# A recurrent attention and four-expert layer on one core: the second chunk's first half goes to seven block products

## The chip, the cores and the metric

The kernel runs on one core of a Trainium2 chip. A core has five engines that each work through their own list of instructions in order: TensorE (PE in the profile; its weight loads stand apart as PEld), VectorE (DVE), ScalarE (ACT), GpSimd (POOL) and SyncE (SP), which here only issues transfers. Transfers (DMAs) run on 16 DMA engines; SP and POOL each feed a queue of them. On-chip memory is SBUF; TensorE writes its results to eight banks of PSUM, and the other engines read them from there. The metric is device time in microseconds (us) of the whole program, the median of several runs.

## The reference, cut to what matters

First a recurrence over the sequence, per batch and head, with gates between 0 and 1; then four experts, weighted by normalised probabilities. All of x is the output of the recurrence, with the heads laid side by side.

```python
f = 1.0 / (1.0 + np.exp(-f_logit))            # B=4, H=8, S=768, D=48
for t in range(S):
    state = f[:, :, t, :, None] * state + np.einsum('bhd,bhe->bhde', k[:, :, t], v[:, :, t])
    y[:, :, t] = np.einsum('bhd,bhde->bhe', q[:, :, t], state)
x = y.transpose(0, 2, 1, 3).reshape(B * S, H * D)        # 3072 x 384
p = domain_probs / (domain_probs.sum(-1, keepdims=True) + 1e-09)
for e in range(4):                                       # w1: 384 x 1024, w2: 1024 x 384
    out += p[:, e:e + 1] * (np.maximum(x @ w1[e], 0.0) @ w2[e])
```

## The kernel before

**Tiles and stages.** The sequence is cut into six chunks of 128 steps (`C = 6`, numbered 0 to 5). A chunk of all four batches gives 512 tokens (`NT`), 128 of each batch. For each chunk the kernel runs an attention part, which gives y of 128 tokens by 384 for each batch, and then the experts on those 512 tokens. Attention of chunk c+1 is woven into the experts of chunk c.

**Attention** (function `attention`) has, per chunk c and batch b, these steps, whose names are used below: `gate1`, `gate2` (ACT), `cs c.b` (running sums of the log gates, PE line L319), `exps` (ACT, L339), `q` and `k` (products with the exponentials, on DVE in the first six batches, else on POOL, L347), `tp` (their transposes: on PE with a copy out of PSUM, L356, or by a transposing DMA, L360), `at` (scores, PE, L383), `ev_at0`, `ev_at1` (masking, DVE, L387), `y` (PE, L394 and L398), `kv` and `ev_kv` (the state, PE L404 and DVE L411) and `sf` (the state's decay, POOL, L416 and L419).

**From y to the experts there are two ways.** In the plain way (chunk 0, and batches 0 and 1 of chunk 1) y is cast to bf16 (`ev_y`), transposed on PE (`xt`, L423), copied out of PSUM to the tile `x` (`ev_xt`), and goes through `h` (first layer, PE L432; relu L441 or L443) and `o` (second layer, PE L447, 8 matmuls of 384 columns for 128 tokens and one expert; `ev_o`, L454, scales by the probability and adds). In the other way (everything from batch 2 of chunk 1 on) the probability is put on y first: since it isn't negative, it passes through the relu. `ev_ys` (ACT L370 or DVE L372) writes y times the probability of one expert; `xs c.b.p` (SP, L375) transposes the two scaled copies of expert pair p by DMA. The first layer is `hs` (PE L464, six matmuls of 256 columns a step, 16 steps for a half chunk and both pairs), its relu `relu_s` (L470, L472). The second layer of two experts is then one product of a 2x2 block matrix (two batches by two experts) with another, and it is done with seven block products instead of eight: `p c.hf.p.m` (PE L501, m = 1 to 7, 8 matmuls of 192 columns each), from sums of hidden blocks `s1` to `s4` (DVE, L482) and sums of weight blocks `t p.1` to `t p.4` (DVE, L491; `t p.3` overwrites a part of the second layer's weights of expert 2p, so all `o` steps of that expert must be done before). `ev_p` (ACT L272 or DVE L509) adds the results up. `store` (SP, L513) writes 128 tokens out. The constant `FAST` (line 166) holds the first chunk and half that go this second way.

**What sets the order.** The program isn't written in its final order. Each step is entered with a cost, a priority and what it depends on; `Plan.run` (line 92) then walks through a model of the engines and fixes, once, in which order each engine gets its instructions and on which of two engines a step runs. Priorities come from the place in the loops and from the long string `MOVES` at the top, which shifts single steps (`name=shift`) or pins their engine (`@DVE`). On the chip every engine takes its instructions strictly in that order. Up to the first `h` the empty time of PE is filled with dummy matmuls (L873).

**The start.** SP loads f, k, q of chunk 0; POOL issues its v (L278) and the weights (L291) in eleven pieces: piece 0 and 1 are the two halves of expert 0's first layer, 2 and 3 those of expert 1, 4 and 5 the second layer of expert 0, and so on. The first expert's first layer in chunk 0 runs in eight units of 12 matmuls with 128 columns, one batch at a time. The weave of chunk 1's attention begins at priority `u0 + 12`.

Of the kernel before, what the change touches and what calls it, by code (L numbers as in the profile page):

```python
# [15 lines left out]
    "k 0.2=46.8@DVE;at 0.1=35.2;ev_xt 0.0=109.8@DVE;ev_at1 0.1=70.1;ev_y 0.3=27.8@ACT;cs 1.0=11.6;at 1.1=19.4;ev_xt 1.0=-4.1@DVE;"  # L16
    "y 1.1=-37.1;ev_ys 1.2.1.1=-9.1;ev_kv 1.3=70.1;ld q2.0=-1.5;ld k2.2=0.2;ld v2.2=15.3;relu 0.0.0.0=-7.7@DVE;h 0.0.0.256=-53.5;"
    "h 0.0.4.256=16.5;o 0.0.0.1=5.7;h 0.1.3.0=25.3;o 0.0.1.1=45.6;o 0.0.3.0=67.2;o 0.1.3.1=6.9;relu 0.3.2.0=15.9@DVE;h 0.3.3.0=-4.2;"
    "h 0.3.6.0=-15.8;o 0.2.3.0=-0.7;h 0.3.7.0=377.1;o 0.2.3.1=-2.5;tp 2.3=-3.5;at 2.1=1.3;ev_ys 2.0.0.0=-60.4@ACT;xs 2.0.1=-2.5;"
    "ev_at0 2.1=-36;ev_at0 2.2=23.5;xs 2.3.0=11.1;kv 2.0=-27.5;sf 2.0.1=-9.9;sf 2.0.3=-58.7;ld f3.0=3.2;o 0.3.1.1=10.5;o 0.3.3.0=-6.7;"  # L20
    "o 0.3.3.1=-22.1;store 0.3.0=20.5;h 1.1.3.0=2.6;o 1.0.1.1=-1;h 1.2.4.0=8.1;h 1.2.5.0=43.5;h 1.3.0.0=-9.1;o 1.2.0.0=19.1;"
    "relu 1.3.1.0=-6.8@ACT;o 1.2.1.0=1.8;h 1.3.3.0=10.5;relu 1.3.7.0=7@DVE;hs 1.1.1.0.0=-39.6;hs 1.1.1.0.4=-28.6;egs 3.1=26.2;"
    "tp 3.1=-56.1;q 3.2=2.6;ev_at0 3.1=7.2;ev_ys 3.1.0.1=20.9;ev_kv 3.0=13.3;kv 3.2=18.7;kv 3.3=10.8;ld q4.0=-7;ld k4.2=14.4;"
    "p 1.1.1.5=-1.3;ev_p 1.1.1.5=-31.6;store 1.2.0=32.2;p 1.1.1.4=5.8;s1 2.0.0=-10.2;hs 2.0.1.0.0=7;relu_s 2.0.1.0.4=1.8@ACT;"
    "p 2.0.0.4=-14.9;s1 2.0.1=2.2;hs 2.1.0.0.0=-31.7;ev_p 2.0.1.1=-60.4;ev_p 2.0.1.2=4.7;hs 2.1.0.0.2=-47.5;relu_s 2.1.0.1.2=2.4@ACT;"
    "hs 2.1.0.0.4=0.4;p 2.0.1.7=10.9;ev_p 2.0.1.3=-15.8;hs 2.1.0.1.6=-2.8;s1 2.1.0=-39.4;s2 2.1.0=2.3;p 2.1.0.1=1.8;p 2.1.0.2=56.5;"
    "ev_p 2.1.0.6=-15.4@DVE;p 2.1.0.5=-1.9;hs 2.1.1.1.6=-3;relu_s 2.1.1.1.6=9.4@DVE;s3 2.1.1=-18;cs 4.0=-6.9;egs 4.0=1.1;q 4.0=0.6;"
    "v 4.1=-4.6;tp 4.1=-14.2;cs 4.2=-65.6;cs 4.3=-4.7;ev_ys 4.0.0.1=-2.9@DVE;ev_ys 4.1.1.0=-89;ev_ys 4.2.1.1=0@ACT;ev_at0 4.3=55.1;"
    "ev_kv 4.1=52.4;kv 4.2=12.3;ld k5.0=7.4;ld f5.2=7.3;ld k5.2=-22.8;hs 3.0.0.0.2=1.4;relu_s 3.0.0.0.2=0@ACT;p 2.1.1.6=17.2;"
    "p 2.1.1.4=17.3;s4 3.0.0=8.2;relu_s 3.0.1.1.0=31.3@DVE;ev_p 3.0.0.2=-39.3;relu_s 3.0.1.0.2=36.2@DVE;p 3.0.0.5=2.3;hs 3.0.1.0.4=2.5;"  # L30
    "relu_s 3.0.1.1.4=8.8@ACT;p 3.0.0.4=3.4;hs 3.0.1.1.6=-5.6;relu_s 3.0.1.1.6=-12.6@DVE;p 3.0.1.1=7.7;hs 3.1.0.1.0=4.3;p 3.0.1.2=0.6;"
    "hs 3.1.0.0.4=-3.5;hs 3.1.0.1.6=2.1;s1 3.1.0=-4.1;s2 3.1.0=-28.8;s3 3.1.0=13.5;hs 3.1.1.0.0=0.4;relu_s 3.1.1.0.0=0@DVE;"
    "hs 3.1.1.1.0=-32.5;hs 3.1.1.1.2=5.9;relu_s 3.1.1.0.4=6.7@DVE;s1 3.1.1=10.8;s2 3.1.1=-19.8;gate1 5.2=-24.6;cs 5.2=-43.5;cs 5.3=10.3;"
    "ev_at0 5.0=-17.9;ev_at1 5.0=-18.3;ev_ys 5.0.0.0=0.1@DVE;ev_ys 5.0.0.1=18.3@DVE;ev_ys 5.1.0.0=-2.7@DVE;ev_ys 5.1.1.0=31.5@DVE;"
# [19 lines left out]
class Plan:  # L54
# [37 lines left out]
    def run(self):  # L92
# [3 lines left out]
        for o in self.ops:  # L96
            if o.name.split(" ")[-1].startswith("0.") and set(o.costs) & {"ACT", "DVE"}:
                o.lag += 0.1
# [41 lines left out]
def kernel(  # L140
# [12 lines left out]
    B, H, S, D = q.shape  # L153
    assert (B, H, S, D) == (4, 8, 768, 48)
    T = 128
# [5 lines left out]
    E, Din, F = moe_w1.shape  # L161
# [383 lines left out]
    for i, (e, which, ks, cols) in enumerate(pieces):  # L545
# [10 lines left out]
        if i == 0:  # L556
            add_v(B - 2, -459.6)
            add_v(B - 1, -459.5)
# [354 lines left out]
```

## Time and profile before

| what | us |
|---|---|
| median of 3 runs (288.75 to 288.84) | 288.76 |
| the profiled execution | 288.44 |
| its span, first to last instruction | 286.7 |
| PE busy, in the span | 280.0 |
| DVE / ACT / POOL busy | 195.5 / 180.7 / 112.0 |
| granted TensorE clock, mean | 1.000 |

The page of a profile gives busy times of each engine, the span cut into 40 slices, the chain of work that ended last (followed back from the last instruction, at each step to what released it), and groups of equal instructions with count, total and mean. A timeline lists instructions in order of time: start, duration, engine, line, operation, output and inputs, shape, and in brackets the idle time before with what ended it. Durations of matmuls there contain the pipeline; from start to start they are shorter, so costs of PE work are taken from the chain, where n matmuls in a row stand with the time that they held the chain.

### The profile page before, as it was taken

What the parts mean: (1) busy time and instruction counts of PE and PEld (TensorE: products, weight loads), DVE (VectorE), ACT (ScalarE), POOL (GpSimd) and SP (SyncE); (2) the same over time, 40 slices, a digit from 0 to 9 for tenths busy, and PEclk for the clock granted to TensorE, in tenths of its full rate; (3) what the DMA queues carried; (4) which work ended last, traced back from release to release, by engine and by line L of the source; (5) the groups of instructions that cost most, each with busy time, mean ns of one, the idle gap of its engine ahead of it and who ended that gap; (6) DMA issues with size and microseconds to landing.
All of it is one profiled execution on the core that took longest, in us unless ns stands there. A gap on an engine that the chain in (4) does not pass through costs nothing.

```text
span 286.7 us, 7475 instructions
## 1 busy us (share of the span) xinstructions
PE 280.0 (98%) x3010; PEld 235.7 (82%) x3016; DVE 195.5 (68%) x385; ACT 180.7 (63%) x343; POOL 112.0 (39%) x181
## 2 busy tenths in 40 slices
PE   7999999999999999999999999999999999999994
PEld 2567555567786999998999999999999999998994
DVE  4595122778698868846889876888885787630683
ACT  5847683758776846867695657375865544659500
POOL 5796500218763762478157258134373000000000
PEclk9999999999999999999999999999999999999999
DMA  7999999997998989999889999995254143420011
GB/s 154 206 173 206 207 195 201 181 198 167 176 184 161 213 154 211 128 222 195 177 182 171 126 219 179 222 184 112 58 132 90 28 84 83 88 56 2 2 55 55
DMA packets 157782, 41.85 MB, mean 146 GB/s; under 512 B 148124, under 2 KB 156956, under 8 KB 157748
## 3 DMA queue, kind: packets, MB, share of 16 engines
q1 hardware_dynamic: 146500, 34.66, 63.7%
q0 software_dynamic: 11248, 6.72, 16.5%
q8 instruction: 23, 0.38, 0.6%
q14 instruction: 11, 0.09, 0.1%
HBM read 31.51 MB, written 4.72 MB: 126 GB/s over the span
## 4 chain that ended last, share of the span: by engine, by line
PE 93%; SPq 2%; DMA 2%; DVE 1%; issue 0%; ACT 0%; DVEq 0%
PE ps_m L464 33%; PE ps_m L501 29%; PE ps_m L447 11%; PE ps_m L432 11%; SPq L282 2%; PE ps_m L383 2%; PE ps_m L398 2%; DMA q<-in_q_dram 2%; PE ps_m L394 1%; PE ps_m L404 1%; PE ps_m L319 1%; PE ps_m L356 1%; DVE AT L387 0%; ACT QK L272 0%; PE ps_m L423 0%
## 5 line engine op out<-in xcount | busy, mean ns | idle before, releaser
L464 PE MATMUL ps_m<-x,w_sb 128*128 128x256 bf16 x864 | 105.6, 273 | 0.0
L472 ACT ACTIVATE h<-ps_m 128x512 bf16<-128x512 f32 x113 | 67.2, 598 | 45.3 <-PE ps_m L464 35.9
L464 PEld LDWEIGHTS <-w_sb 128*128 128x128 bf16 x864 | 82.9, 98 | 9.1
L501 PEld LDWEIGHTS <-S 128*128 128x128 bf16 x576 | 48.6, 98 | 1.1
L509 DVE TENSOR_TENSOR o<-ps_m,o 128x192 f32<-128x192 f32 x91 | 31.2, 354 | 20.0 <-PE ps_m L501 17.7
L482 DVE TENSOR_TENSOR S<-h 128x1024 bf16<-128x1024 bf16 x36 | 28.2, 800 | 13.0 <-ACT h L472 12.9
L501 PEld LDWEIGHTS <-h 128*128 128x128 bf16 x432 | 36.3, 98 | 0.9
L447 PE MATMUL ps_m<-w_sb,h 128*128 128x384 bf16 x192 | 36.1, 326 | 0.0
L432 PE MATMUL ps_m<-x,w_sb 128*128 128x128 bf16 (+2 forms) x260 | 35.6, 281 | 0.2
L443 ACT ACTIVATE h<-ps_m 128x512 bf16<-128x512 f32 (+1 forms) x49 | 24.6, 512 | 14.0 <-PE ps_m L432 12.9
L387 DVE TENSOR_TENSOR AT<-ps_m,mask 128x512 bf16<-128x512 f32 x48 | 30.5, 683 | 4.1 <-PE ps_m L383 3.8
L419 POOL TENSOR_TENSOR Sf<-Sf,egs 48x192 f32<-48x192 f32 x40 | 20.7, 521 | 28.4 <-DVE Sf L411 23.9
L339 ACT ACTIVATE e<-ps_m 128x384 f32<-128x384 f32 x48 | 26.9, 671 | 6.3 <-PE ps_m L319 2.9
L470 DVE TENSOR_SCALAR h<-ps_m 128x512 bf16<-128x512 f32 x31 | 21.0, 691 | 12.9 <-PE ps_m L464 10.3
L432 PEld LDWEIGHTS <-w_sb 128*128 128x128 bf16 x264 | 21.8, 98 | 9.4
L347 POOL TENSOR_TENSOR qk<-q,e 128x384 bf16<-128x384 f32 x19 | 24.1, 1271 | 13.7 <-ACT e L339 6.3
L501 PE MATMUL ps_m<-ts_sb,S 128*128 128x192 bf16 x288 | 28.7, 246 | 0.0
L501 PE MATMUL ps_m<-w_sb,S 128*128 128x192 bf16 x288 | 28.5, 246 | 0.0
L501 PE MATMUL ps_m<-w_sb,h 128*128 128x192 bf16 x288 | 28.4, 246 | 0.0
L447 PEld LDWEIGHTS <-h 128*128 128x128 bf16 x192 | 18.3, 98 | 11.9 <-issue 0.4
L370 ACT ACTIVATE yb<-ps_m,pn 128x384 bf16<-128x384 f32 x49 | 26.1, 584 | 2.8 <-PE ps_m L398 2.7
L347 POOL TENSOR_TENSOR qk<-k,e 128x384 bf16<-128x384 f32 x19 | 19.4, 1023 | 14.7 <-DVE Sf L411 4.0
(74 smaller groups left out, 308.7 us busy)
## 6 DMA issues: line engine op xcount, KB each, us to landing
out_dram<-o SPq DMA_DIRECT2D x23, 192.0 KB, 2.2
w_sb<-in_moe_w_dram POOLq DMA_DIRECT2D x5, 768.0 KB, 17.3
k<-in_k_dram SPq DMA_DIRECT2D x10, 384.0 KB, 5.5
q<-in_q_dram SPq DMA_DIRECT2D x10, 384.0 KB, 5.6
v<-in_v_dram SPq DMA_DIRECT2D x10, 384.0 KB, 5.6
f<-in_f_logit_dram SPq DMA_DIRECT2D x9, 384.0 KB, 4.9
w_sb<-in_moe_w_dram POOLq DMA_DIRECT2D x6, 384.0 KB, 8.7
f<-in_f_logit_dram SPq DMA_DIRECT2D x6, 192.0 KB, 3.8
```

The source lines that it names most:

```text
L339: nc.scalar.activation(out=o, in_=i, func=AF.Exp, scale=1.0 if j else -1.0)
L347: return engines[eng].tensor_tensor(out=tl("qk", c, b)[:, j, :, 0:D].rearrange("t (i r) d -> t i r d", r=2), in0=tl("qk"[j], c, b // 2)[:, ...
L370: nc.scalar.activation(out=ys, in_=y, func=AF.Copy, scale=pe)
L387: nc.vector.tensor_tensor(out=tl("AT", c, b)[:, r].rearrange("s i t -> s (i t)"), in0=tl("A", c, b, r).rearrange("s i t -> s (i t)"), in1= ...
L432: nc.tensor.matmul(out=hp(c, e, fc, n0, n1, nf)[:, f], lhsT=w1_sb[:, e, kk, (fc + f) * 128:(fc + f + 1) * 128], rhs=tl("xT", c)[:, kk, n0: ...
L443: nc.scalar.activation(out=dst, in_=src, func=AF.Relu)
L447: nc.tensor.matmul(out=tl("op", c, e, nt, part)[:, cols], lhsT=tl("h", c, e, half_of(c, nt * T))[:, fc, nt * T:(nt + 1) * T], rhs=w2_sb[:, ...
L464: nc.tensor.matmul(out=out_[:, f], lhsT=w1_sb[:, e, kk, (fc + f) * 128:(fc + f + 1) * 128], rhs=tl("xs", c, hf, p)[:, el, kk, :], start=(k ...
L472: nc.scalar.activation(out=dst, in_=tl("hp", c, hf, p, el, fc), func=AF.Relu)
L482: return nc.vector.tensor_tensor(out=s(j), in0=in0, in1=in1, op=op)
L501: nc.tensor.matmul(out=out_, lhsT=lhs[:, fc, :], rhs=rhs[:, fc, :], start=(first and fc == 0), stop=(fc == KF - 1), skip_group_check=True)
L509: nc.vector.tensor_tensor(out=o, in0=src, in1=o, op=ALU.add)
```

## The change

Four things change besides the priorities.

1. `FAST` becomes `(1, 0)`: batches 0 and 1 of chunk 1 also take the second way. Their `ev_y`, `xt` and `ev_xt` go, eight `ev_ys` and four `xs` come. The loop for chunk 1 issues two more groups of 16 `hs` steps in place of 32 `h` units of 256 columns, 14 block products in place of the 16 `o` steps of two halves each, and `t_sums()` before them all.
2. The first expert's first layer in chunk 0 runs in batches of two, one and one: hidden blocks 0 to 3 for batches 0 and 1 together (256 columns), then for batch 2, blocks 4 to 7 for batches 0 to 2 together (384 columns), then all for batch 3.
3. v of batch 2 is issued before the first weight piece instead of after it; the weave of chunk 1's attention starts at `u0 + 6`; a delay of 0.1 that the model put on ACT's and DVE's steps of chunk 0 is gone.
4. `MOVES` is another string from beginning to end (it is left out here but for a line), so the order differs on every engine in every chunk. Among others the loads of chunk 1's second half come as f, q, v, k instead of f, k, q, v; `k 0.0` and `q 0.1` move from POOL to DVE; and the last two block products and stores at the end change places.

```diff
 MOVES = (
-    "k 0.2=46.8@DVE;at 0.1=35.2;ev_xt 0.0=109.8@DVE;ev_at1 0.1=70.1;ev_y 0.3=27.8@ACT;cs 1.0=11.6;at 1.1=19.4;ev_xt 1.0=-4.1@DVE;"
+    "ld q1.2=-2.1;ld v1.2=-4.1;q 0.0=-31.7@DVE;k 0.0=-82.1@DVE;q 0.1=3@DVE;k 0.1=2.9@DVE;ev_tp 0.1=-31.7@ACT;k 0.2=10.7@DVE;tpk 0.2=6.6;"
...
-        for o in self.ops:
-            if o.name.split(" ")[-1].startswith("0.") and set(o.costs) & {"ACT", "DVE"}:
-                o.lag += 0.1
...
-    FAST = (1, 1)
+    FAST = (1, 0)
...
-    for i, x in enumerate("f0 k0 q0 f1 k1 q1 f2 f3 k2 q2 v0 k3 q3 v1".split()):
+    for i, x in enumerate("f0 k0 q0 f1 k1 q1 f2 f3 k2 q2 v0 k3 q3 v1 v2".split()):
...
         if i == 0:
-            add_v(B - 2, -459.6)
             add_v(B - 1, -459.5)
...
-            base, slope = {0: (u0 + 12, 5), 1: (u0 + B1, S1)}.get(c, (u0 + B2, S2))
+            base, slope = {0: (u0 + 6, 5), 1: (u0 + B1, S1)}.get(c, (u0 + B2, S2))
...
         if c == 0:
-            for b, fc in ((0, 0), (1, 0), (0, 4), (1, 4), (2, 0), (2, 4), (3, 0), (3, 4)):
-                zip_units([(c, 0, fc, b * T, (b + 1) * T, [b], 4)], [])
+            for fcs, n0, n1, xs, nf in ((range(0, KF // 2), 0, N2, LO, 1), (range(0, KF // 2, 2), N2, NT - T, [2], 2),
+                                        (range(KF // 2, KF), 0, NT - T, LO + [2], 1), (range(0, KF, 4), NT - T, NT, [3], 4)):
+                zip_units([(c, 0, fc, n0, n1, xs, nf) for fc in fcs], [])
             unit[0] = u0 + 2 * KF
         elif c == 1:
-            zip_units([], ol(0, E - 1, ALL))
-            zip_units(hl(c, 0, 0, N2, LO), [])
-            for e in range(1, E):
-                zip_units(hl(c, e, 0, N2, LO), ol(c, e - 1, LO))
             t_sums()
-            zip_groups((c, 1, 0), None, ol(c, E - 1, LO))
+            zip_groups((c, 0, 0), None, ol(0, E - 1, ALL))
+            zip_groups((c, 0, 1), (c, 0, 0))
+            zip_groups((c, 1, 0), (c, 0, 1))
             zip_groups((c, 1, 1), (c, 1, 0))
             prev = (c, 1, 1)
```

The instruction order of the changed program around the first steps of chunk 1 is as follows. PE: `at 1.0, at 1.1, o 0.3.0.0, o 0.3.1.0, y 1.0, kv 1.0, o 0.3.2.0, y 1.1, kv 1.1`, five more halves of `o 0.3` with `cs 1.2` and `cs 1.3` among and after them, then `hs 1.0.0.0.0`. DVE: `ev_at0 1.0, ev_at1 1.0, ev_at0 1.1, ev_at1 1.1, relu 0.3.7.0, ev_kv 1.0, ev_ys 1.1.0.0, ev_kv 1.1, ev_ys 1.1.0.1, ev_o 0.3.0.0`. SP: the four loads of chunk 1's second half, `xs 1.0.0`, the store of batch 0 of chunk 0, `xs 1.1.0`, the store of batch 1, `xs 1.0.1`, `xs 1.1.1`.

Farther on, PE: `cs 2.0, y 1.2, kv 1.2, cs 2.1, p 1.0.0.5, y 1.3, kv 1.3`, the products 6, 2, 3, 7 and 4 of the first pair, `cs 2.3, cs 2.2`, the products 1, 2 and 5 of the second pair, then `hs 1.1.0.0.0`. ACT: `exps 2.0, ev_ys 1.2.0.0, exps 2.1, ev_ys 1.2.0.1`. SP: `xs 1.2.0, tp 2.0, xs 1.2.1, xs 1.3.0, xs 1.3.1`.

## The prediction

> **What bounds the kernel now.** I read the page first, for the engine that is never idle, then the chain, then matmul groups by shape, and last timelines where the change cuts in.
>
> ```profile
> PE 280.0 (98%) x3010; PEld 235.7 (82%) x3016; DVE 195.5 (68%) x385; ACT 180.7 (63%) x343; POOL 112.0 (39%) x181
> ...
> PE   7999999999999999999999999999999999999994
> ...
> PE 93%; SPq 2%; DMA 2%; DVE 1%; issue 0%; ACT 0%; DVEq 0%
> ```
>
> PE is busy in every slice but the first and last, and the chain that ended last is PE for 93%. So work taken off PE is worth its full time, and each new wait of PE costs its full time. What a matmul costs is read from the chain, where n in a row stand with the time they held it:
>
> ```profile
> 22.57 1.34 PE ps_m L432 x24
> ...
> 33.21 1.30 PE ps_m L447 x8
> ...
> 102.49 1.31 PE ps_m L464 x12
> 103.80 0.66 PE ps_m L501 x8
> ```
>
> That is 0.056 us for 128 columns, 0.163 for 384, 0.109 for 256, 0.0822 for 192 (0.658 for eight). The cut in chunk 1 needs rows of what stands between y and the second way's first layer:
>
> ```profile
> 18.29 0.40 PE L383 MATMUL ps_m<-QK 48*128 48x128 bf16 x8 [0.30 <-ACT QK L272]
> ...
> 59.01 2.48 DVE L387 TENSOR_TENSOR AT<-ps_m,mask 128x512 bf16<-128x512 f32 x4
> ...
> 63.13 0.74 DVE L411 TENSOR_TENSOR Sf<-Sf,ps_m 48x192 f32<-48x192 f32 x2 [0.25 <-PE ps_m L404]
> ...
> 83.00 0.21 PE L394 MATMUL ps_m<-sb,QK 112*128 112x96 bf16 x1
> ...
> 87.07 1.24 SPq L375 DMA_TRANSPOSE x<-yb  x1
> ...
> x<-yb SPq DMA_TRANSPOSE x36, 2.8
> ```
>
> The last three lines tell most: y of batch 3 in chunk 1 begins at 83.00, its first transposed, scaled x is issued at 87.07 and lands 2.8 later, at 89.87. From y to x it is 6.87 us. PE had 7.7 us of other work in between (the next L464 begins at 90.71), so nobody saw it.
>
> **The change, part by part.** All sums are against the profiled execution, 288.44 (span 286.7); the median, 288.76, lies 0.32 above it.
>
> *PE work.* Second layer of chunk 1's first half: 64 matmuls of 384 columns go, 64 x 0.163 = 10.43; 14 block products x 0.658 = 9.21 come: -1.22. Six transposes of y go: 6 x 0.056 = -0.34. The first expert: 96 x 0.056 = 5.38 becomes 36 x 0.056 + 12 x 0.109 + 12 x 0.163 = 5.28: -0.09. First layer of chunk 1: 96 matmuls of 256 columns either way, nothing. Sum -1.65.
>
> *The start.* Before, expert 1's first matmul begins at 25.77, with one unit of expert 0 (0.67) still undone; with the 0.09 above, equal work is reached at 26.35. After, no unit is left over. Its first unit with 384 columns needs the second weight piece, which the trace has landing at 21.79, and v of batch 2 moves only past the first piece, so that stays. From there 4.14 us of matmuls stand before expert 1: 25.94, so -0.4. It can't be much better, since the weights hold it; it is worse by up to 1 if x of batches 0 and 1, which the first unit now needs together, come late. The masks of batch 3 (DVE, 19.03 to 20.32 before) have as many DVE steps ahead of them as before, so I keep -0.4. The products moved to DVE and the PSUM copies moved to ACT hide behind loads: DVE waited 1.6 us for q of batch 2 before, and ACT must lose that much first; uncovered they would cost some 0.6.
>
> *First wait: `hs 1.0.0.0.0` needs x of batches 0 and 1.* From the start of `y 1.1` to it, PE has y 0.38, kv 0.17, five o halves 3.25, two cs 0.33: 4.13 us. The path from y to x took 6.87 above: a wait of 2.7. Counted out from `at 1.0` along DVE's order: mask starts 0.74 after at (18.29 to 19.03), four masks 2.39, one relu 0.61, ev_kv 0.77, ev_ys 0.53, ev_kv 0.77, ev_ys 0.61: 6.42. The transpose of batch 1 then stands on SP behind the store of batch 0, which waits for the `ev_o` behind that ev_ys: +0.53, issue of the store +0.37, transpose to landing +2.8: 10.1. PE's work from `at 1.0` to hs is 7.22: a wait of 2.9. I take 2.8. Bounds: were nothing of DVE's between (0.59 from y to the first ev_ys at 83.59, two of them 1.15, 2.8), it is 4.54 - 4.13 = 0.4; with the longest landing of these transposes, 5.0, it is 5.1. Behind hs all of PE's list waits, and DVE runs dry after its four weight sums.
>
> *Second wait: `hs 1.1.0.0.0` needs x of batches 2 and 3.* PE's work from `y 1.3` to it is now 0.38 + 0.17 + five products 3.29 + two cs 0.33 + three products 1.97 = 6.14: by the 6.87 a wait of 0.7. Counted along the queues: on ACT two exps and two ev_ys (0.42 + 1.13 + 0.47 + 1.13 + 0.58) end 2.2 us after y 1.3 starts; then SP issues `xs 1.2.0`, `tp 2.0`, `xs 1.2.1`, each 1.34 apart, and only then `xs 1.3.0`: 6.25 + 2.8 = 9.05, a wait of 2.9. Ahead of it product 5 waits for DVE's s1, which stands behind a late relu; that overlaps. From below nothing. I take 1.8, the middle, as each row holds for a part of the path.
>
> *Load on DVE and ACT.* Eight s sums 8 x 0.77, 14 ev_p x 0.35, eight ev_ys x 0.6 come: 15.9; eight ev_o x 0.61, 12 x 0.42 + 20 x 0.39 of relus less 16 x 0.64, and two casts and two copies 1.7 go: 9.2. So 6.7 more on two engines. In 66.12 to 90.71 they were busy 19.7 and 19.2 of 24.6, so there is room for it, beside PE: nothing, and up to 2 if it bunches on DVE.
>
> *The end.* Before, both halves of the last results came after PE's last product (283.15, two of 0.62 together), then a store of 192 KB, 2.2 to landing. After, one ev_p follows and the last store is 96 KB, 1.6 to landing: 0.27 + 0.6, less since the 192 KB store is issued just before: -0.5 (bounds 0 and -0.8).
>
> *The rest of `MOVES`* reorders chunks 2 to 5. PE idled about 1.0 us in all after 66 us, so there is little to win; I take 0, up to 0.5 either way.
>
> *Sum:* -1.65 - 0.4 + 2.8 + 1.8 - 0.5 = +2.05: 290.5 as profiled, 290.8 on the median's scale.
>
> [...]
>
> **Rivals.**
> - *Both x come in time, and it is faster.* If DVE, ACT and SP reach the steps earlier than my rows say, the first wait is its lower bound 0.4 and the second nothing: 290.8 - 4.2 = 286.6. For it: 36 transposes in the trace never stop PE visibly. Against: those had 7.7 us of cover, here 4.13 and 6.14. It decides for faster when both waits together stay under 2.5.
> [...]
> - *DVE becomes the bound in chunk 1.* If the 6.7 us fall mostly on DVE, 19.7 + 4 of 24.6 is nearly full, and products wait for s sums beyond the second wait: +1.7, 292.5.
>
> **How the numbers follow.** My case, waits of 3.4 (2.7 + 0.7) to 5.8 (both queue counts) together, 289.6 to 292.0: 0.5. Faster rival 0.2; waits in between (2.2 to 3.4), which land near no change, 0.08; DVE-bound 0.12; clock 0.1. Within 0.2% (288.2 to 289.3), about what a measurement of this kernel can tell from no change: 0.1, from the in-between case and the faster rival's upper part; faster then 0.17, slower 0.73. The range runs from 287.6, inside the faster rival, to 293.4, which takes in DVE-bound and stops short of the clock's: some 0.1 is left out at each end.
>
> **What would show it.** A PE gap of 2 to 3 us just before the first L466 (the old L464), at about 66 us, ended by a DMA of x; a second, of 1 to 3, some 20 us later at the first hs of the second half, again ended by x; 128 matmuls of 384 columns and 1120 of 192; expert 1 starting near 25.9; 0.3 to 0.6 less after the last product. I am wrong if PE stays closed at both places, if the gaps are ended by DVE or ACT instead, or if the granted clock drops after one.

## The result, and the profile after

The changed kernel takes 297.81 us (median of 4 runs, 296.91 to 298.28) against 288.80 (288.75 to 289.04) of the kernel before: a ratio of 1.0307, with a 95% interval of 1.0281 to 1.0332. The direction of the prediction was right; the size was not. 290.8 was forecast, and the time lies 4.4 us above the top of the range.

The profiled execution took 297.67. The page of the changed kernel, with the answers to the rows shown of before (span, busy times, slices of PE and of its granted clock, the chain's shares, and the group of the scaled first layer):

```profile
span 296.0 us, 7501 instructions
...
PE 280.6 (95%) x3016; PEld 237.7 (80%) x3022; DVE 201.1 (68%) x394; ACT 181.9 (61%) x339; POOL 114.3 (39%) x182
...
PE   6889999997986899999999999999999999999995
...
PEclk9999999997999999999999999999999999999999
...
PE 78%; DMA 7%; DVE 5%; ACT 2%; POOL 2%; issue 2%; SPq 2%; ACTq 0%; DVEq 0%
...
L466 PE MATMUL ps_m<-x,w_sb 128*128 128x256 bf16 x960 | 121.2, 275 | 5.3 <-DMA x<-yb 4.1
```

Three things differ. PE, busy in all middle slices before, is open in the tenth, twelfth, thirteenth and fourteenth (a slice is 7.4 us, so from 66 to 103 us) and a little in the second and third. The granted clock drops in one slice (7 in the tenth, 9 in all others). And the chain that ended last is PE for 78% of its length, no longer for 93%: part of the rest is the start, as before, but most of it now lies between 59 and 101 us and goes through DVE, POOL, DMA and ACT. By `hs 2.0.0.0.0` the kernel is 7.35 us late (116.26, before 108.91), and at the end of the last matmul 9.31 (292.42 and 283.11). The tails behind that are about equal, 3.5 and 3.6.

What PE waited for from 57 to 110 us, in the view of waits, changed kernel (before, the same view is empty):

```profile
PE ps_m L466 <- DMA x<-yb: 4.1, 2, 2.1
PE ps_m L466 <- ACT e L341: 0.8, 1, 0.8
PE ps_m L503 <- DVE o L511: 0.6, 1, 0.6
PE ps_m L449 <- DMA w_sb<-in_moe_w_dram: 0.5, 1, 0.5
PE ps_m L321 <- ACT gp L317: 0.3, 1, 0.3
PE ps_m L503 <- ACT e L341: 0.3, 1, 0.3
```

The first row is the two waits of the prediction. The others it didn't have. In the timeline of PE, the two waits and what followed each:

```profile
69.06 9.70 PE L466 MATMUL ps_m<-x,w_sb 128*128 128x256 bf16 x72 [2.00 <-DMA x<-yb]
78.69 0.73 PE L385 MATMUL ps_m<-QK 48*128 48x128 bf16 x16
...
94.53 2.14 PE L466 MATMUL ps_m<-x,w_sb 128*128 128x256 bf16 x18 [2.08 <-DMA x<-yb]
...
100.70 0.82 PE L466 MATMUL ps_m<-x,w_sb 128*128 128x256 bf16 x6 [0.84 <-ACT e L341]
```

The 72 matmuls at 69.06 take 9.70; at 0.109 each they are 7.85. The stretches show why (length, then busy time of PE, PEld, DVE, ACT, POOL, the granted clock, DMA share, GB/s; each stretch 3.41 long, changed kernel):

```profile
65.93:69.35 3.42, 1.42 (x10) 0.75 (x9) 3.42 (x6) 2.26 (x4) 2.61 (x4) 1.00 0.72 189
69.35:72.76 3.41, 3.41 (x18) 2.37 (x17) 3.34 (x4) 1.19 (x2) 3.18 (x2) 0.50 0.66 130
72.76:76.17 3.41, 3.41 (x33) 3.04 (x32) 1.21 (x1) 2.99 (x5) 3.36 (x5) 1.00 0.53 123
```

In the 3.41 us after the gap the granted clock was 0.50 (18 matmuls in it, 33 in the next stretch), a loss of 1.77. In the stretch from 72.76 on it was 1.00 again.

**Where the time came from.** I laid the steps of the program onto both traces. Idle in these sums is counted from the end of PE's work at its cost from start to start, so that a wait comes out a little longer than in the brackets above (2.16 and 2.25 for 2.00 and 2.08).

| difference of the two profiled executions, by PE | us |
|---|---|
| PE work taken off | -1.65 |
| start: expert 1 at 26.72, equal work before at 26.35 | +0.4 |
| before `o 0.3.0.0` (60.27): a weight piece lands late | +0.6 |
| `cs 1.3` to `hs 1.1.0.0.0`: idle 6.44 and half rate 1.77, less 0.09 before | +8.1 |
| after `hs 1.1.0.0.0` to `hs 2.0.0.0.0` (mostly at 100.70) | +1.0 |
| later, 1.99 of idle against 0.69 | +1.3 |
| sum | +9.8 |
| measured, end of the last matmul | +9.31 |

I haven't found the place of the 0.5 between the sum and the measurement. The bulk is one stage, `cs 1.3` to `hs 1.1.0.0.0`:

| | before | after |
|---|---|---|
| stage, us | 25.41 (65.31 to 90.71) | 27.80 (66.73 to 94.53) |
| PE's own work in it | 25.32 | 19.59 |

In both kernels batch 3 of chunk 1 goes, in this time, through `cs 1.3`, its exponentials, four products on POOL, the transpose `tp 1.3`, `at 1.3`, four masks, `y 1.3`, `ev_ys`, the transpose `xs 1.3.0`, and on to `hs 1.1`. That takes about 25 us. Before, PE had 25.3 us of other work meanwhile, and nothing of the chain could be seen. After, it has 19.6. The timeline of PE before, at the start, the middle and the end of the stage:

```profile
65.14 0.49 PE L319 MATMUL ps_m<-gp,Ub 128*128 128x384 bf16 x2
...
78.62 0.62 PE L383 MATMUL ps_m<-QK 48*128 48x128 bf16 x16
...
90.71 2.79 PE L464 MATMUL ps_m<-x,w_sb 128*128 128x256 bf16 x24
```

The 16 matmuls in the middle are `at 1.2` with `at 1.3` right behind it. The pair begins at 78.62 before and at 78.69 after, although PE had 13.2 us of work ahead of it before and 8.0 after. Before, the transposes for it had landed by 77.02. After, `tp 1.3` lands at 78.98 and `at 1.3` begins at 79.02; `xs 1.3.0` lands at 94.49 and `hs 1.1` begins at 94.53. So at both places PE starts as the chain's transfer lands. What went out from under the chain (5.7) is: four products now behind `hs 1.1` (2.6), two `o` steps now ahead of `cs 1.3` (1.3), the saving of the second layer itself (1.2), steps of chunk 2 (0.6). The chain that ended last, changed kernel (start, duration, what):

```profile
59.24 0.38 PE ps_m L385 x8
59.61 2.48 DVE AT L389 x4
...
69.58 0.91 POOL qk L349
70.49 0.77 issue
...
76.15 5.10 DMA f<-in_f_logit_dram
81.27 0.84 ACT f L313
...
83.12 0.32 PE ps_m L321
...
95.96 3.43 DMA egs<-e
100.70 0.38 PE ps_m L466 x2
```

The chain leaves PE at 59.61 and comes back to it at 83.12; in between it is DVE (masks, state, scaled copies, weight sums), POOL's products, and transfers. Before, PE held 93% of the whole chain. Two pieces are not of batch 3 at all: f of chunk 2 is issued at 76.15, behind `tp 1.3` on SP (before, at 62.19), and the copy `egs 2.0` (POOL, 95.96) holds a tile that the exponentials need, which hold a PSUM bank that `hs 1.1.0.1.4` needs. (That second wait belongs to this execution: a second trace of the same kernel, in part C, has none there.)

### The profile page after: what moved, and what is told of

Its sections match the earlier page's. It is cut to its first block, busy times and chain, and to the rows that moved or that the text cites. A ratio compares the mean times of both kernels' runs of the same rounds, so it can differ in the third digit from the quotient of the medians.

```text
span 296.0 us, 7501 instructions
## 1 busy us (share of the span) xinstructions
PE 280.6 (95%) x3016; PEld 237.7 (80%) x3022; DVE 201.1 (68%) x394; ACT 181.9 (61%) x339; POOL 114.3 (39%) x182
## 4 chain that ended last, share of the span: by engine, by line
PE 78%; DMA 7%; DVE 5%; ACT 2%; POOL 2%; issue 2%; SPq 2%; ACTq 0%; DVEq 0%
PE ps_m L466 31%; PE ps_m L503 29%; PE ps_m L434 7%; PE ps_m L449 5%; DMA w_sb<-in_moe_w_dram 2%; SPq L284 2%; DMA f<-in_f_logit_dram 2%; DMA k<-in_k_dram 1%; PE ps_m L385 1%; PE ps_m L400 1%; DMA egs<-e 1%; PE ps_m L396 1%; PE ps_m L406 1%; POOL qk L349 1%; ACT e L341 1%
## 5 line engine op out<-in xcount | busy, mean ns | idle before, releaser
L466 PE MATMUL ps_m<-x,w_sb 128*128 128x256 bf16 x960 | 121.2, 275 | 5.3 <-DMA x<-yb 4.1
L466 PEld LDWEIGHTS <-w_sb 128*128 128x128 bf16 x960 | 92.8, 99 | 17.4 <-DMA x<-yb 4.7
L511 DVE TENSOR_TENSOR o<-ps_m,o 128x192 f32<-128x192 f32 x101 | 34.7, 352 | 30.8 <-PE ps_m L503 28.1
L503 PEld LDWEIGHTS <-S 128*128 128x128 bf16 x640 | 53.8, 98 | 1.7
L472 DVE TENSOR_SCALAR h<-ps_m 128x512 bf16<-128x512 f32 x42 | 28.7, 689 | 13.9 <-PE ps_m L466 12.7
L372 ACT ACTIVATE yb<-ps_m,pn 128x384 bf16<-128x384 f32 x56 | 29.8, 584 | 4.3 <-PE ps_m L400 2.5
L349 POOL TENSOR_TENSOR qk<-q,e 128x384 bf16<-128x384 f32 x18 | 22.4, 1248 | 15.7 <-DMA q<-in_q_dram 9.2
L445 ACT ACTIVATE h<-ps_m 128x512 bf16<-128x512 f32 (+2 forms) x33 | 18.4, 559 | 9.5 <-PE ps_m L434 8.5
L434 PE MATMUL ps_m<-x,w_sb 128*128 128x512 bf16 (+3 forms) x128 | 23.3, 319 | 0.9 <-DMA w_sb<-in_moe_w_dram 0.7
L449 PE MATMUL ps_m<-w_sb,h 128*128 128x384 bf16 x128 | 22.9, 326 | 0.5 <-DMA w_sb<-in_moe_w_dram 0.5
L274 ACT COPY o<-ps_m 128x192 f32<-128x192 f32 x35 | 11.2, 319 | 14.4 <-PE ps_m L503 13.6
```

The lines of the kernel that those rows point to most:

```text
L349: return engines[eng].tensor_tensor(out=tl("qk", c, b)[:, j, :, 0:D].rearrange("t (i r) d -> t i r d", r=2), in0=tl("qk"[j], c, b // 2)[:, ...
L372: nc.scalar.activation(out=ys, in_=y, func=AF.Copy, scale=pe)
L434: nc.tensor.matmul(out=hp(c, e, fc, n0, n1, nf)[:, f], lhsT=w1_sb[:, e, kk, (fc + f) * 128:(fc + f + 1) * 128], rhs=tl("xT", c)[:, kk, n0: ...
L449: nc.tensor.matmul(out=tl("op", c, e, nt, part)[:, cols], lhsT=tl("h", c, e, half_of(c, nt * T))[:, fc, nt * T:(nt + 1) * T], rhs=w2_sb[:, ...
L466: nc.tensor.matmul(out=out_[:, f], lhsT=w1_sb[:, e, kk, (fc + f) * 128:(fc + f + 1) * 128], rhs=tl("xs", c, hf, p)[:, el, kk, :], start=(k ...
L472: nc.vector.tensor_relu(out=dst, in_=tl("hp", c, hf, p, el, fc))
```

## Experiments

Theory A, after the result: chunk 1 is bound by the chain of batches 2 and 3, and the work that the edit takes off PE there is taken out of that chain's cover; each wait is its own cost. Theory B: the drop of the clock behind the first gap is what makes the loss larger than forecast. Theory C: a few steps stand badly in the new order (loads on SP, the copy on POOL) and can be put right one by one. Theory D: the cost is not chunk 1's but the new priorities' or the start's. Several expectations set a rival against A, that DVE, ACT and POOL are simply full in chunk 1; it is taken up at the end of part A.

In the edits below, "x < y" means that step x is put ahead of step y on its own engine, all else in the order of the changed kernel. Line numbers in traces of kernels with long lists are up to 50 higher, so the scaled first layer can be L514 there, the products of blocks L551, the running sums L369.

### B: the clock, and the first gap

Ten dummy matmuls of 512 columns fill PE while it waits for the first x.

```diff
+        for _ in range(FILL.get((c, hf, p, el, fc), 0)):
+            nc.tensor.matmul(out=tl("hp", c, hf, p, el, fc), lhsT=w1_sb[:, 0, 0, 0:128], rhs=w1_sb[:, 0, 0, 0:512], start=True, stop=True)
...
+FILL = {(1, 0, 0, 0, 0): 10}
```

> The changed kernel, with ten dummy 512-column matmuls (0.2165 us each in the trace, 2.17 together) put in PE's list ahead of hs 1.0.0.0.0, into its own PSUM bank, so that PE is busy in the first gap (66.89 to 69.06) while x is under way. Theory 'clock': the half rate recorded from 69.35 to 72.76 comes from PE's idle 2.16 us; with the filler the granted clock stays at 1.0 after 66 us and the time falls by the half of 3.4 us, some 1.7, to about 296.0 where the clock had fallen. Rival: the fall has another cause, and the same spell stands in the records at the same place: 297.7, no change. Either way the wait itself stays: hs begins at 69.0 to 69.2.

Measured: 299.53, ratio 1.0358 (1.0311 to 1.0404). The stretches of this kernel, at the first place and at the second:

```profile
69.35:72.76 3.41, 3.41 (x34) 3.06 (x32) 3.38 (x3) 3.12 (x6) 3.41 (x3) 1.00 0.69 133
...
91.53:94.94 3.41, 1.23 (x15) 1.00 (x13) 3.39 (x7) 0.27 (x1) 3.21 (x5) 1.00 1.15 133
94.94:98.36 3.42, 3.42 (x17) 2.36 (x17) 0.00 (x0) 1.19 (x2) 2.55 (x6) 0.50 0.93 177
```

The first gap is filled and the granted clock is 1.00 behind it, but PE then waits at the scores of batch 3, which had been hidden by the slow spell (timeline, same kernel):

```profile
79.71 0.40 PE L385 MATMUL ps_m<-QK 48*128 48x128 bf16 x8 [2.90 <-DMA QK<-qk]
```

The slow spell came back behind the second gap (2.18 us; 0.50 from 94.94 to 98.36). So this run couldn't price the spell alone. The same filler in the best order found further down (`e16_f3`) did:

> The kernel with fifteen moves (f of chunk 3 early) and ten dummy 512-column matmuls (2.17 us) ahead of hs 1.0.0.0.0, in its own bank. The gap of 2.76 us at 65.7 shrinks to about 0.6. [...]

Measured: 295.40 (7 runs), ratio 1.0214 (1.0192 to 1.0237), against 295.44 of the same order without filler, 1.0204 (1.0152 to 1.0255). The mean clock of its profiled execution is 0.999, where one spell of 3.41 us at 0.50 would make 0.994, so it has none of that length; `at 1.2` begins at 77.69 instead of 78.14, but `at 1.3` at 78.50 instead of 78.38, and `hs 1.1` at 90.73 instead of 90.59. What the slow clock took, PE here spent waiting for the same transfers. The two intervals leave room for a price of about 1 us. Theory B falls even so: two of the four runs of the changed kernel had a mean clock of 1.000, and they took 296.91 and 297.95, still 8 and 9 us more than the kernel before.

### C: single steps

Second wait: SP transposes the first x of batch 3 sooner.

```diff
+        ("xs 1.2.1", "xs 1.3.1"),
+        ("tp 2.0", "xs 1.3.1"),
```

> The changed kernel, with only SP's order altered: xs 1.3.0 now ahead of xs 1.2.1 and tp 2.0. Theory 'queue': in the changed kernel's trace xs 1.3.0 is issued at 90.94 though its source was written by about 88.8; behind xs 1.2.0 alone (done 88.14) it goes out at 88.8 to 89.0 and lands at about 91.7, so the second gap (2.25 us at 92.20) falls under 0.3, and the time by about 2.0, to 295.7; if chunk 2's later steps are the next limit, the gap at 99.64 (1.03) grows by what is won. Rival 'load': DVE and ACT write x's source too late themselves; then the gap stays at 1.5 or more and the time within 0.7 of 297.8.

Measured: 298.79, ratio 1.0329 (1.0285 to 1.0374). `xs 1.3.0` was issued at 88.39 instead of 90.94 and `hs 1.1` began at 91.90 instead of 94.53, without a wait. The waits of PE from 57 to 110 us in this kernel:

```profile
PE ps_m L385 <- DMA QK<-qk: 2.6, 2, 1.7
...
PE ps_m L466 <- ACT e L341: 1.7, 1, 1.7
```

The second wait is gone. From 6 us behind the start of `hs 1.1` on, PE waits for a transpose of chunk 2 and then for exponentials instead (1.08 at `at 2.1`, 1.91 at 98.06, in the count from start to start), and there is a wait of 1.7 at `at 1.3` ahead of it.

The late f of chunk 2: its loads go ahead on SP (`ld f2.0 < xs 1.0.0`, `ld k2.0 < tp 1.2`, `ld q2.0 < tp 1.2`); then the gates, sums and exponentials of chunk 2's first batches go ahead too (`gate1 2.0`, `gate2 2.0 < relu_s 1.0.0.0.0`; `cs 2.0 < hs 1.0.0.0.4`, `cs 2.1 < hs 1.0.1.1.0`; `exps 2.0`, `exps 2.1` ahead of the relus there).

> The changed kernel, with three loads of chunk 2 earlier in SP's order: f of batches 0 and 1 ahead of the first scaled transpose of chunk 1 (SP idles from 61.4 to 63.9 there), k and q ahead of tp 1.2. Theory 'late load': f lands before 68 instead of at 81.25, gate1 and gate2 on ACT run where they stand with no wait (1.88 us of idle before), cs 2.0 no longer holds PE (0.47 at 82.53), ACT reaches exps and ev_ys of chunk 1's second half some 0.5 to 1.5 sooner and the second gap shrinks by as much: 296.3 to 297.2. Cost: the first wait grows if the load lies ahead of the first transpose (up to 0.3). Rival 'load on DVE and ACT': 297.5 to 298.2, the 0.47 comes back at the next products.

> As the kernel with the three earlier loads, and also gate1, gate2, exps of chunk 2's batches 0 and 1 earlier in ACT's list and cs 2.0 and cs 2.1 earlier in PE's (behind the second, and the sixth, hs of chunk 1), where ACT idles between relus. Theory 'order of chunk 2's front': ACT is then free when y 1.2 ends, ev_ys 1.2.0.1 ends about 1.5 to 2 sooner than 86.69, the second gap (2.25) falls to 0.5 to 1.0, POOL's products and the egs transfers follow sooner and the gap at 99.64 (1.03) goes: 294.0 to 295.3. Rival 'load on DVE and ACT': the waits only change their place, 296.5 to 298.

Measured: 299.75, ratio 1.0368 (1.0312 to 1.0423), and 299.35, ratio 1.0342 (1.0303 to 1.0382). The wait for f is gone in both. The first gap grew to 3.55 and 4.20 us, with f's load now ahead of `xs 1.0.0` on SP, and waits of 0.3 to 2.2 stayed behind it.

The copy on POOL (`egs 2.0 < sf 1.2.0`, `egs 2.1 < sf 1.2.0`), then six moves together, which add `ld f2.0 < xs 1.0.0`, `store 0.0.0 < ld f2.2`, `xs 1.2.1 < ld q2.2`, `cs 2.0 < hs 1.0.1.1.4`:

> The changed kernel with two small transfers moved in POOL's list: egs 2.0 and egs 2.1 ahead of sf 1.2.0 (they were issued at 95.96 in its trace, behind POOL's sf steps, and ACT's exps 2.2 waited 2.17 us for them). Theory 'PSUM bank held through egs': exps 2.2 runs some 5 us sooner, the bank comes free, the gap at 99.64 (1.03) goes: 0.7 to 1.1 less than the changed kernel on the same chip. Rival 'any gap comes back at the next step': within 0.4 of it.

> The changed kernel with four orders moved together: f of chunk 2 ahead of the first scaled x, the store of the first rows behind chunk 2's q, the x for the second pair of experts behind xs 1.3.0 and tp 2.1, egs 2.0 and 2.1 ahead of sf 1.2.0; and cs 2.0 one step earlier on PE. (a) 'several orders hold PE in turn': 2 to 3.5 less than the changed kernel on the same chip, 294.5 to 296. (b) 'DVE, ACT and POOL are full': within 1 of it.

and, on the same chip, the changed kernel again, nothing edited, to see how far a single trace can be trusted:

> The changed kernel as it is, on the chip of the three runs above. Both theories: 297 to 299, ratio 1.03 to 1.035.

Measured: 297.57, ratio 1.0298 (1.0262 to 1.0333); 296.46, ratio 1.0264 (1.0243 to 1.0285); unedited 297.85, ratio 1.0296 (1.0256 to 1.0335). With the copy moved there is no wait at 100 us, but there is none in the unedited kernel's second trace either, so the move can't be given the credit; the time is the same. In that second trace the gaps are 2.67, 1.83 and 3.01 with the slow spell behind the last (mean clock 0.994): the shares of the waits move from run to run. The six moves together are 1.4 us below the unedited kernel on the same chip, with intervals that overlap. So of single waits I read only where they are, and trust medians for what they cost.

### A: the chain itself

The chain of batches 2 and 3 is moved forward as a whole, 34 moves: gates, running sums, exponentials, POOL's products, transposes, `at 1.3`, masks, y, scaled copies, `xs`.

> The changed kernel with the steps of chunk 1's second half moved forward in each engine's list, nothing removed: gate and exps of batches 2 and 3 ahead of ev_ys on ACT, cs 1.2 and 1.3 two to five steps earlier on PE, POOL's four products ahead of sf 1.1.0, tp 1.2 and tp 1.3 ahead of the transposes for the second pair of experts, at 1.3 and the four masks ahead of the late relus, y 1.2 and y 1.3 between the hs steps, and their xs ahead of tp 2.0. Theory 'one chain': the four runs before took away single waits (idle before the first hs, the last x behind tp 2.0, the late f) and each time the idle came back at the next step (for example 1.91 and 3.09 us at at 1.3), since the steps from cs 1.3 over exps, POOL's products, tp 1.3, at 1.3, masks, y 1.3, ev_ys and xs 1.3.0 to hs 1.1.0.0.0 take 28 us and PE has about 23 us of other work meanwhile. Moved forward by some 5 us the chain no longer ends last: the waits at at 1.3, at cs 2.0 and before hs 1.1.0.0.0 (2.25) and the one at 99.64 (1.03) go, the first wait stays: 293.0 to 294.8. Rival 'DVE and ACT are overloaded in chunk 1': the same work takes the same time, 296.5 or more.

Measured: 309.94, ratio 1.0727 (1.0660 to 1.0795). It was worse, and a part of the chain did not move. The timeline of POOL:

```profile
70.48 1.72 POOL L395 TENSOR_TENSOR qk<-k,e 128x384 bf16<-128x384 f32 x1 [4.78 <-issue]
```

The products waited 4.78 for DVE's weight sum `t 1.1`, and then took 1.7 to 1.9 each beside the next ones. (The program itself makes a product on POOL wait for the sum or product on DVE that stands ahead of it in the planned order; in the changed kernel the issue waits of the chain above are such turns.) The next two take the four weight sums off that place, alone and together with a second form of the moved chain:

```diff
+    "t 1.1<ev_p 1.0.0.3;t 1.2<ev_p 1.0.1.5;t 1.3<ev_p 1.0.1.6;t 1.4<ev_p 1.0.1.7"
```

> The changed kernel with one thing moved: DVE's four weight sums t 1.1, t 1.3, t 1.2, t 1.4 (68.34 to 73.98 in its trace) go later in DVE's list, each to just before the product that needs it. In that trace POOL's products k 1.2, q 1.3, k 1.3 stand beside them: k 1.2 starts 0.95 late, just as t 1.1 ends, and they take 1.71, 1.90 and 1.71 instead of the 1.00, 1.20 and 1.00 of the kernel before. Theory 'POOL's products hold the second half': they end about 2.5 to 3 sooner (71.9 instead of 74.8), tp 1.3 and the f of chunk 2 behind it on SP are issued as much sooner, at 1.3 finds its data (at most 0.3 of wait), and the time falls by 1.5 to 2.5: 295.5 to 296.5; what the sums then push on DVE after 86 may take back up to 1. Rival: POOL is hidden and the wait at at 1.3 has another cause: 297.5 or more.

> The second attempt at moving chunk 1's second half forward, after the first one cost 12 us because POOL's k 1.2 waited for t 1.1 all the same (4.78 us) and SP's transposes for the second pair of experts stood behind tp 1.2. Now the weight sums t 1.* come late, POOL's four products come right behind exps 1.2, tp 1.2 and tp 1.3 go out behind the two first x, chunk 2's f, k, q come before xs 1.2.0, and all hs of the first pair run ahead of those of the second. Theory 'one chain': tp 1.3 lands at 72 to 73, at 1.3, cs 2.0, hs 1.1.0.0.0 and the step at 99.6 no longer wait (together about 4.5 us in the changed kernel's trace) and hs 1.0.0.0.0 still waits 2 to 3 us: 292 to 294. Rival 'DVE and ACT are overloaded in chunk 1': 296.5 or more, with PE stopped by DVE's or ACT's steps between 78 and 92.

Sums late alone: 301.44, ratio 1.0440 (1.0422 to 1.0457). Its POOL and SP in the timeline:

```profile
69.66 1.19 POOL L397 TENSOR_TENSOR qk<-q,e 128x384 bf16<-128x384 f32 x1
70.81 1.00 POOL L397 TENSOR_TENSOR qk<-k,e 128x384 bf16<-128x384 f32 x1
...
72.98 3.13 SPq L410 DMA_TRANSPOSE QK<-qk  x1
```

The last three products were done at 71.8 instead of 74.8, at 1.0 and 1.2 us each, the rates of the kernel before; but the issue of `tp 1.3` then took 3.13 instead of 1.24, so `at 1.3` gained next to nothing, and the sums, put later on DVE, made products wait there (1.80 at 87.4) and the exponentials' bank (3.56 at 99.74).

With the chain: 303.11, ratio 1.0503 (1.0477 to 1.0529). Here the chain did move: `tp 1.3` issued at 69.34 (74.86 in the changed kernel), `at 1.2` and `at 1.3` from 73.73 (78.69), `y 1.3` at 79.82 (84.66). There was no wait before `hs 1.1`. It began at 93.94 all the same, 0.6 earlier, because PE now waited elsewhere; the waits from 57 to 115 us in this kernel:

```profile
PE ps_m L514 <- ACT e L389: 4.7, 1, 4.7
PE ps_m L514 <- DMA x<-yb: 2.4, 2, 1.4
PE ps_m L551 <- DVE o L559: 1.5, 1, 1.5
```

A's own forecasts failed in both kernels that moved the chain (293.0 to 294.8 against 309.94, 292 to 294 against 303.11). What the chain is moved past on DVE, ACT, POOL and SP falls behind by as much or more. The rival, that these engines are full, had said 296.5 or more, and the times lie there. But the traces don't show full engines. In the changed kernel's stage of 27.80 us DVE is busy 22.4, ACT 18.7 and POOL 17.4, and DVE and ACT stand idle waiting for PE (timelines of DVE and of ACT, changed kernel):

```profile
77.48 0.69 DVE L472 TENSOR_SCALAR h<-ps_m 128x512 bf16<-128x512 f32 x1 [3.51 <-PE ps_m L466]
```

```profile
95.40 1.91 ACT L474 ACTIVATE h<-ps_m 128x512 bf16<-128x512 f32 x3 [3.81 <-PE ps_m L466]
```

In the kernel with the sums late DVE even idles 7.37 us there (68.5 to 75.9). So, for the order that was given, the traces show that PE starts at `at 1.3` and at `hs 1.1` when the chain's transfers land; that the chain's length alone sets the loss is argued from the stage's sums and not shown, since no run shortened the chain without putting something else behind.

Fourteen small moves, on all queues at once:

```diff
+    "ld f2.0<xs 1.0.0;xs 1.2.1<ld v2.2;exps 2.1<gate1 2.2;hs 1.0.1.1.6<hs 1.0.0.1.4;hs 1.0.0.1.6<hs 1.0.1.1.6;"
+    "p 1.0.0.7<p 1.0.0.2;relu_s 1.0.1.0.4<ev_p 1.0.0.7;ev_p 1.0.0.3<ev_p 1.0.1.2;egs 2.0<sf 1.2.1;t 1.3<s1 1.0.0;"
+    "ev_p 1.0.0.6<ev_ys 1.3.0.0;s4 1.0.0<relu_s 1.0.1.0.4;hs 1.0.1.0.4<p 1.0.0.7;store 0.0.0<store 0.2.0"
```

> The changed kernel with fourteen single moves in the engines' lists between 57 and 100 us, chosen from the waits in the traces: f of chunk 2 ahead of the first x, xs 1.2.1 behind xs 1.3.0, egs 2.0 ahead of sf 1.2.1, the hs of the second pair of experts and product 7 of the first interchanged with steps that wait, two ev_p and one s sum earlier or later, the store of the first rows later. No step is removed or added. (a) 'several orders hold PE in turn': 4 to 5.5 less than the changed kernel on the same chip, 292.5 to 294; the first wait (2 us) and the late head remain. (b) 'DVE, ACT and POOL are full': 296 or more.

Measured: 296.43, ratio 1.0277 (1.0238 to 1.0316). `hs 1.1` now begins at 90.73, where it began before the change, and `hs 1.1.0.1.4` at 96.16 (100.70). A part of what was won was lost again 20 us later, in the gates of chunk 3, whose f had been loaded late (timelines of ACT and of PE):

```profile
119.77 0.84 ACT L361 ACTIVATE f<-f 128x768 f32<-128x768 f32 x1 [2.83 <-DMA f<-in_f_logit_dram]
```

```profile
121.54 0.53 PE L369 MATMUL ps_m<-gp,Ub 128*128 128x384 bf16 x2 [1.83 <-ACT gp L365]
```

The next adds `ld f3.0 < ld k3.0`; the one after is another set of 14 moves, with y of batch 0 ahead of second-layer steps of chunk 0 (`o 0.3.1.0 < o 0.3.2.0`, `ev_kv 1.1 < ev_o 0.3.0.0`, `o 0.3.0.0 < o 0.3.0.1` and others).

> The kernel with the fourteen moves and one more: f of chunk 3 (batches 0 and 1) ahead of k of chunk 3 on SP, so that it is issued at about 98.6 instead of 114.0. If the gain was given back there, the 2.00 us wait at cs 3.0 (119.43 in that trace) goes and the time falls by 1.5 to 2: 294.4 to 295. If later orders hold PE again: within 0.5 of 296.4.

> Another set of fourteen moves in the changed kernel, of which two aim at the first wait: y 1.0 and kv 1.0 come right behind at 1.1 and the o steps that stood there (o 0.3.0.0, o 0.3.1.0) come behind y, so that they cover the path from y to x; further f of chunks 2 and 3 early, xs of the second pair later, egs 2.0 earlier, three hs steps of the second pair moved. Theory 'orders': the first wait falls from 2.2 to 3.1 us to 0.5 to 1.5, hs 1.1.0.0.0 begins at 88.5 to 90.5, the time is 291.5 to 294.5. Rival 'DVE, ACT and POOL are full in chunk 1': 296 or more.

Measured: 295.44 (294.34 to 295.66), ratio 1.0204 (1.0152 to 1.0255), and 296.19, ratio 1.0219 (1.0162 to 1.0276; the ratio leaves out a run of 300.14, without which the median is 295.76). The wait for f is gone, and in the first of them a wait of 1.7 at `at 2.3` (109.24) is there instead. In the second the wait before `hs 1.0.0.0.0`, at which two of the moves aimed, is still 1.96. In the first the stage `cs 1.3` to `hs 1.1` takes 24.94 with the same 19.59 of PE work: 5.35 still idle or slowed. Moves alone, then, bring back some 2.4 of the 9.0 us (by the ratios 3.0), and no version with the new chunk 1 ran as fast as the kernel before. For the two sets of 14 moves the rival of the full engines had said 296 or more, and A's side 292.5 to 294 and 291.5 to 294.5; the times lie at the rival's end.

### D: the parts of the change

Chunk 1's first half as before, the rest of the change kept (start, priorities):

```diff
-    FAST = (1, 0)
+    FAST = (1, 1)
...
+            zip_units([], ol(0, E - 1, ALL))
+            zip_units(hl(c, 0, 0, N2, LO), [])
+            for e in range(1, E):
+                zip_units(hl(c, e, 0, N2, LO), ol(c, e - 1, LO))
             t_sums()
-            zip_groups((c, 0, 0), None, ol(0, E - 1, ALL))
-            zip_groups((c, 0, 1), (c, 0, 0))
-            zip_groups((c, 1, 0), (c, 0, 1))
+            zip_groups((c, 1, 0), None, ol(c, E - 1, LO))
```

> The changed kernel with one part undone: chunk 1's first half again by x transposed on PE, 256-column first layers and 384-column second layers, as before; first expert's batches, load order and the new priorities stay (those of steps that no longer exist drop out). Theory 'chunk 1's edit costs it': 289 to 292, as PE has its other work again beside the second half's chain, and only the head (0.8 late) and the priorities remain. Rival 'the new priorities or the head cost it': 295 or more.

Measured: 293.12, ratio 1.0146 (1.0124 to 1.0169). In 57 to 110 us PE doesn't wait at all in this kernel. With the edit of chunk 1 it is 297.81, so that edit costs 4.7 under the new priorities. Without any priorities, `MOVES` empty, the new structure and the old:

> The changed kernel with its table of priorities left empty, to be set against the kernel before with an empty table. Theory 'chunk 1's edit costs it whatever the priorities': this is 4 to 9 us slower than its counterpart. Rival 'only the new table costs it': the two are within 2 us, or this one is faster by the 1.65 us of PE work that it saves.

> The kernel before with its table of priorities left empty, the counterpart of the run above. Both theories: slower than the kernel before, by an amount that is the worth of its table; I expect 3 to 10 us (292 to 299).

Measured: 302.25, ratio 1.0468 (1.0443 to 1.0493), and 291.32, ratio 1.0107 (1.0064 to 1.0151). The whole change but its priorities costs 10.9 when nothing is arranged, and 9.0 with each one's own arrangement. The waits lie in the same stage; the view of waits from 57 to 110 us of the new structure without priorities:

```profile
PE ps_m L437 <- DMA x<-yb: 10.5, 1, 10.5
```

The first hs waits 10.5 us for x when nothing is arranged around it (L437 is the scaled first layer here). The new priorities take most of that one wait away, and leave others behind it; the kernel gains 4.4 us by them in all (302.25 to 297.81), the kernel before 2.5 by its own (291.32 to 288.8).

The start alone, in the kernel before (batches by two, one and one; v of batch 2 ahead of the first weights):

```diff
-    for i, x in enumerate("f0 k0 q0 f1 k1 q1 f2 f3 k2 q2 v0 k3 q3 v1".split()):
+    for i, x in enumerate("f0 k0 q0 f1 k1 q1 f2 f3 k2 q2 v0 k3 q3 v1 v2".split()):
...
-            add_v(B - 2, -459.6)
...
-            for b, fc in ((0, 0), (1, 0), (0, 4), (1, 4), (2, 0), (2, 4), (3, 0), (3, 4)):
-                zip_units([(c, 0, fc, b * T, (b + 1) * T, [b], 4)], [])
+            for fcs, n0, n1, xs, nf in ((range(0, KF // 2), 0, N2, LO, 1), (range(0, KF // 2, 2), N2, NT - T, [2], 2),
+                                        (range(KF // 2, KF), 0, NT - T, LO + [2], 1), (range(0, KF, 4), NT - T, NT, [3], 4)):
+                zip_units([(c, 0, fc, n0, n1, xs, nf) for fc in fcs], [])
```

> The kernel before with the head's part alone: the first expert's first layer by two, one and one batches and v of batch 2 ahead of the first weights; all of PE's list behind chunk 0's first expert is unchanged. My prediction had -0.4 for it. In the changed kernel's trace expert 1 begins at 26.72 with nothing left over, where equal work in the kernel before is reached at 26.35, since the first matmul waits 0.67 us for the first weights (20.16), which now come behind v: by that 0.4 to 0.8 slower than before, 289.2 to 289.7. If later waits take it up: no change, within 0.2 of 288.8.

Measured: 289.93 (10 runs) against 289.44 (13 runs), ratio 1.0012 (0.9988 to 1.0036). Expert 1 begins at 26.64 there, against 26.35 for equal work before, and the last matmul ends 0.36 later. The interval holds no change; the trace says some 0.3 slower, not faster. So of theory D the start explains some 0.4. The rest of it, 293.12 with the old way of chunk 1, is 4.3 above the kernel before, but those priorities were made for other steps. Its trace (293.74) has PE waiting 1.45 for the first weight piece (20.57), 1.1 between 160 and 200 us and 1.7 after 250. Of that the changed kernel's trace has 0.67 at the first weight piece and 0.3 in the later chunks, so by the waits, most of these 4.3 are no share of the 9.0.

## Why the prediction was wrong in size

The step that failed is the pricing of the open stage: two waits of 4.6 together, each laid against a short stretch behind y, where the whole stage from `cs 1.3` to `hs 1.1` lost 8.1. Of the 7.0 us between forecast and measurement, that is 3.5; the rest of `MOVES`, put at nothing, makes 2.9, the start 0.8 and the end 0.4. These add up to 7.6; the difference is the 0.5 that I couldn't place.

**PE work.** Right as counted: the groups show 128 matmuls of 384 columns and 1120 of 192, and the stage lost the work it should. What failed is the sentence in front of it, that work taken off PE is worth its full time. It was read from a chain that is PE for 93%, but that is the chain of a kernel in which PE's work just covers a second chain (25.32 of 25.41). Of the -1.65, the -1.22 of the second layer lay in that cover; by these sums it was worth nothing.

**First wait.** Predicted 2.8, measured 2.16 (2.00 in the brackets). The count along DVE's order was good: from `at 1.0` to the first hs 10.1 counted, 9.89 measured; PE work from y to hs 4.13 and 4.12.

**Second wait.** Predicted 1.8, measured 2.25, and 1.48 more of waits ahead of it on the same stretch, at products that wanted a PSUM bank or a result of DVE. From `y 1.3` to `hs 1.1` it took 9.87, where the queue count had said 9.05 and the row 6.87: the queue count was the better row, and taking the middle was the mistake. PE's work there was as counted (6.14, measured 6.15).

**What the sum left out.** Two waits were laid against short stretches, y to x. The stage has to be laid out whole, 25 to 28 us of chain against 19.6 of work. Had I put the work left on PE from `cs 1.3` to `hs 1.1` against the 25.4 that the stage took before, there would have been 5.8 instead of 4.6; the chain then grew by 2.4 more, which makes the 8.2. The terms missed are the one at `at 1.3`, which the slow spell covered (1.77), the wait for f of chunk 2 (0.47), and the 1.48.

**Rest of `MOVES`, 0 up to 0.5.** By the places of the waits it came to some +2.9, though no run prices these alone (0.6 before `o 0.3.0.0` for a weight piece, 1.0 mostly at 100 us for a PSUM bank, 1.3 later). I had argued from the idle time that could be won, not from the loads that the new order puts elsewhere (f of chunk 2 issued 14 us later, `egs` behind the state on POOL).

**Start and end.** Predicted -0.4 and -0.5; +0.4 and -0.1. At the start the first `h` units waited 0.67 at 20.16 for the first weight piece, which now stands behind v of batch 2 on POOL: I had kept expert 1's bound by the second piece and costed v's move at nothing.

**Load on DVE and ACT.** Costed at nothing; neither is full over the stage, but from 66 to 74 us DVE is busy 7.9 of 8, against 6.7 before, with the weight sums in it. That is a piece of the chain, not a bound of its own: with the sums taken away from there (`e10_tlate`) the kernel was slower.

**The clock.** The prediction gave a fall of the clock 0.1. Here a gap of 2.00 us was followed by 3.41 us at a granted clock of 0.50, and by the prediction's own last line a drop of the granted clock was a sign of being wrong. Which gaps such a spell follows was not shown: the changed kernel's second gap, of 2.08, had none behind it, nor had the first gap in `e2_xs` (2.50) and in `e10_tlate` (2.49). The price of a fall that lies behind the 0.1 and the upper end of the range is shown by no run; in its place the changed kernel's trace shows 1.77 of PE's time, and `e19_f3_fill` no measurable part of the kernel's.

**Open.** Of the 9.0 us, moves recovered 2.4 to 3.0. Whether an order exists in which this structure loses nothing, I can't say: `e9_chain2` shows that the chain can be 5 us earlier, at the cost of other steps. How much of the 4.3 us of `e6_old_chunk1` comes from priorities that were made for another structure is open too.

## What to carry to other kernels

An engine that is never idle can still be only just long enough to cover a second chain: before pricing work taken off it, lay the longest chain of the stage, from end to end, against what the engine still has to do in that time. Where the cover goes, waits turn up one behind the other, and mending the one that is seen only shows the next; a gap in one trace says where to look for the chain, not what it costs. And if the priced steps are moved past loads or small copies on other queues, follow what those feed two stages later.

## What the runs showed of the hardware that I had not expected

**The granted clock behind a gap.** In the changed kernel's trace, between the start and the last matmul, it was 0.50 from 69.35 to 72.76, behind a gap of 2.00 us, and 1.00 elsewhere, also behind the second gap, of 2.08. In `e1_fill` it was 0.50 from 94.94 to 98.36, behind a gap of 2.18. In `e14_many`, with 2.92 before the first `hs`, it was 0.59 from 69.35 to 72.76 and 0.91 in the 3.41 us after that; in `e7_new_no_priorities`, where PE waited 10.54 there, 0.74 and 0.50 in the same two stretches. But in `e2_xs` and `e10_tlate`, with 2.50 and 2.49 before the same `hs`, it was 1.00 in both stretches, and the 72 matmuls that took 9.70 in the changed kernel took 8.03; farther on in `e2_xs` it was 0.60 from 98.36 to 101.80, with a gap of 1.72. So in these traces the length of the gap doesn't tell whether the clock falls. Two of the four runs of the changed kernel had a mean clock of 1.000 (296.91 and 297.95 us; the others, at 0.992 and 0.988, took 297.67 and 298.28); those two have no trace, so what PE's gaps were there isn't shown.

**POOL beside DVE.** The same product of 128x384 on POOL took 1.00 before (k) and 1.71 in the changed kernel beside DVE's weight sums; with the sums moved away (`e10_tlate`) it was 0.99 to 1.00 again.

**Issues of transposing transfers.** SP's issue of `tp 1.3` took 1.24 in the changed kernel and 3.13 in the one where it came two us sooner (`e10_tlate`), so that the time won on POOL was lost on the queue. What held it, the traces here don't show.
